# A decode-attention kernel: two ring slots exchanged, the load of x moved to the sync queue, and the last row of W_down read by sixteen small transfers

## The chip, the cores and the metric

The kernel runs on one core of a Trainium2 chip. The metric is device time in microseconds (us), the median of several executions. A profile is one traced execution. Its span (first to last instruction) is 1.8 to 1.9 us shorter than the time of the same execution.

The profile of the kernel before was taken from an execution of 382.86 us, 1.2 us above that kernel's median.

## The reference

One decoding step of a transformer block, with batch 4 and one query token: layer norm of x, a q projection with wq, attention over the last 4096 positions of a K and V cache with 16 KV heads of 128, the output projection wo, and a gated MLP.

```python
W = min(4096, max(256, Sk // 4))                       # 4096
k = jnp.repeat(k_cache[:, :, Sk - W:, :], rep, axis=1) # v likewise
scores = jnp.einsum("bhqd,bhkd->bhqk", q, k) * (Dh ** -0.5)
p = _softmax(scores, axis=-1)
o = jnp.einsum("bhqk,bhkd->bhqd", p, v)
...
h  = x + _A_ref(_layernorm(x), k_cache, v_cache, wq, wo)
h2 = h + _B_ref(_layernorm(h), W_gate, W_up, W_down)   # last product: W_down
```

K and V make 16 tiles each of 4 MB (K0..K15, V0..V15). With the weights, 159.8 MB have to be read. Nothing is read twice.

## The kernel before

A helper records every operation; `P.dma("sync", ...)` issues a load on the sync queue, in program order. K, V and the main part of wq share a ring of four slots of 4 MB. `place` makes a load wait for the last reader of the bytes that it overwrites.

```python
def place(name, off, size, reader, make, key=None):
    deps = []                       # readers of what lay at off..off+size
    ...
    P.dma("sync", ("L",) + name, make, semk, deps)

def add_kv(kind, g):
    s = ring_slot()                 # next of the four slots
    ...
    place((kind, g), off, TILE, ("QK", g, 1) if kind == "K" else ("PV", g), ...)

add_kv("K", 0)                      # slot s
s = ring_slot()                     # slot s+1
place(("wq", 0), wq_off, TILE, "QMM", ...)      # freed by the q projection
P.dma("sync", ("L", "wq", 1), ...)              # wq's last 64 rows, no slot
for g in range(1, NTILE):           # K1, K2, K3 (slot of K0), K4 (slot of wq),
    add_kv("K", g)                  # V0, K5, V1, K6, V2, K7, ...
    if g >= 4:
        add_kv("V", g - 4)
...                                 # wo, W_gate, W_up, V's last tiles
for j in range(4):                  # W_down, 4 blocks of 9 rows per partition
    for r0, r1 in ((0, 9),) if j < 3 else ((0, 6), (6, 9)):
        place(("wd", j, r0), ...)
...
P.dma("scalar", ("L", "x"), lambda e: e.dma_start(out=x_bf[:, :], in_=A_x...), "d_x")
dve("bn0", bn_stats of x_bf)        # waits for x
...                                 # layer norm, transposes of x, xnT
turn_k(0, 0)                        # VectorE transposes the two halves of K0
turn_k(0, 1)
pe_q(); act_q(); dve_q(); put_q(0)  # q projection; q copied where QK reads it
```

VectorE executes in program order (QK(g) are the score matmuls of tile g, PV(g) those with V): in e8, below, K0's first transpose is put ahead of the layer norm and runs at 13.18 us, while the second, behind it, runs at 27.62. So x's layer norm stands ahead of the transposes of K0, these ahead of the copy of q, and that ahead of the first score matmuls QK(0). QK(0) releases K0's slot.

Of the kernel before, what the change touches and what calls it, by code (L numbers as in the profile page):

```python
# [12 lines left out]
D = 576  # L13
# [107 lines left out]
def bass_sequential_preLN__sliding_block_cached__glu_gated_reglu__decode_kernel(  # L121
# [12 lines left out]
    with ExitStack() as es:  # L134
        cnt = [0]

        def sb(name, shape, dt):
            return es.enter_context(nc.sbuf_tensor("sb_" + name, shape, dt))

        P = Prog()  # L140
# [7 lines left out]
        arena = sb("arena", [128, AW], BF16)  # L148
# [23 lines left out]
        x_bf = sb("x_bf", [B, D], BF16)  # L172
# [47 lines left out]
        def place(name, off, size, reader, make, key=None):  # L220
            deps = []
            for blk in range(off // 64, (off + size) // 64):
                r = owner.get(blk)
                if r is not None and r not in deps:
                    deps.append(r)
                owner[blk] = reader
            semk = key or "d_" + "_".join(str(v) for v in name)
            P.dma("sync", ("L",) + name, make, semk, deps)
            land[name] = off

        ring = [(-1 - 2 * NTILE) % NSLOT]

        def ring_slot():
            s = ring[0] % NSLOT
            ring[0] += 1
            return s


        def add_kv(kind, g):
            b, qd = divmod(g, 4)  # L240
            s = ring_slot()
            off = slot0 + s * TILE
            cache = A_k_cache if kind == "K" else A_v_cache
            src = cache[b, 4 * qd:4 * qd + 4, SK - WIN:SK, :].rearrange("a (p t) d -> p a (t d)", p=32)
            place((kind, g), off, TILE, ("QK", g, 1) if kind == "K" else ("PV", g),
                  lambda e: e.dma_start(out=arena[:, off:off + TILE], in_=src), key=f"slot{s}")


        def main_rows(W):
            return W[0:512, :].rearrange("(p r) n -> p (r n)", r=4)  # L250

        def last_rows(W):
            return W[512:576, :].rearrange("r (a n) -> (r a) n", a=2)

        add_kv("K", 0)
        s = ring_slot()
        wq_off = slot0 + s * TILE
        place(("wq", 0), wq_off, TILE, "QMM",
              lambda e: e.dma_start(out=arena[:, wq_off:wq_off + TILE], in_=main_rows(A_wq)), key=f"slot{s}")
        P.dma("sync", ("L", "wq", 1), lambda e: e.dma_start(out=pT[:, 0:2048], in_=last_rows(A_wq)), "d_wq1")  # L260
        for g in range(1, NTILE):
            add_kv("K", g)
            if g >= 4:
                add_kv("V", g - 4)
# [16 lines left out]
        wd_off = []  # L281
        for j in range(4):
            wd_off.append(off)
            for r0, r1 in ((0, 9),) if j < 3 else ((0, 6), (6, 9)):
                place(("wd", j, r0), off + r0 * D, (r1 - r0) * D, "DOWN",
                      lambda e, off=off, j=j, r0=r0, r1=r1: e.dma_start(  # L286
                          out=arena[:, off + r0 * D:off + r1 * D],
                          in_=B_W_down[j * 1152:(j + 1) * 1152, :].rearrange("(p r) n -> p (r n)", p=128)[:, r0 * D:r1 * D]))
            off += WDJ


        pool("c_idb0", lambda e: e.memset(ident_b[:, :], 0.0))
# [21 lines left out]
                                                in_=c_qm[:, :, :].rearrange("p q (h j) -> p q h j", j=4),  # L314
# [34 lines left out]


        act("warm_sqrt", lambda e: e.activation(out=warm[:, 0:1], in_=eps_c[:, :], func=ACT.Sqrt), ["c_eps"])
        P.dma("scalar", ("L", "x"), lambda e: e.dma_start(out=x_bf[:, :], in_=A_x.rearrange("b s d -> (b s) d")), "d_x")
        for hf in range(2):
            dve(f"bn{hf}", lambda e, hf=hf: e.bn_stats(out=bn[:, hf, :], in_=x_bf[:, hf * 288:(hf + 1) * 288]),
                [("L", "x")] if hf == 0 else [])
# [263 lines left out]
        for a in range(8):  # L619
            for j in range(4):  # L620
                for n in range(2):
# [7 lines left out]
                                             in_=bass.AP(tensor=psb, offset=512 + 224, ap=[[4096, 128], [1, 64], [0, 2]])), ["part1"])  # L629
# [28 lines left out]
        for g in range(2):  # L658
            for c in (4, 0, 1, 2, 3):
                off = gu_off[(g, c // 4)]  # L660
                for m in range(3):
                    for j in range(4):
                        first = m == 0 and j == 0 and c % 4 == 0
# [30 lines left out]
        for j in range(4):  # L694
            wv = arena[:, wd_off[j]:wd_off[j] + WDJ].rearrange("p (r n) -> p r n", n=D)
            for r in range(9):
                for n in range(4):
                    deps = []
                    if n == 0 and (r == 0 or (j == 3 and r == 6)):
                        deps = [("L", "wd", j, r)] + (["HC0", "HC1", "HC2"] if j == 0 else [])  # L700
                    pe("DOWN", lambda e, j=j, r=r, n=n, wv=wv: e.matmul(  # L701
                        bank[0][32 * n:32 * n + 32, 0:144], lhsT=hhT[:, r * 128 + 32 * j:r * 128 + 32 * j + 32],
                        rhs=wv[:, r, 144 * n:144 * (n + 1)], start=False, stop=(j == 3 and r == 8), skip_group_check=True), deps)
        dve("OUT", lambda e: e.tensor_copy(out=out_sb[:, :], in_=bank[0][:, 0:144]), ["DOWN"])
        orow = out.rearrange("b s d -> (b s) d")
        for n in range(4):
            P.dma("sync" if n % 2 == 0 else "scalar", ("O", n),
                  lambda e, n=n: e.dma_start(out=orow[:, 144 * n:144 * (n + 1)], in_=out_sb[32 * n:32 * n + 4, :]), f"d_out{n}", ["OUT"])
# [30 lines left out]
```

## Time and profile before

| what | before |
|---|---|
| time | 381.62 us (381.42 to 381.76, 3 executions) |
| bytes read | 159.8 MB at a mean of 419 GB/s |
| steady rate | 432 GB/s, one 4 MB tile every 9.71 us |
| x landed, QK(0) began | 2.4 us, 31.35 us |
| last W_down transfer landed on its last engine | 377.55 us of a span of 381.1 |

From the page of the kernel before: the span, TensorE's granted clock (as a share of full speed) in tenths, the DMA engines' busy share in tenths, and what they moved, each in 40 slices of 9.5 us, and the line of the load queue.

```profile
span 381.1 us, 3671 instructions
PEclk9998999989978897798997887989989956756687
DMA  8999999999999999999999999999999999999993
GB/s 331 440 423 421 406 440 437 433 428 427 420 439 440 424 433 426 433 430 435 433 430 427 435 430 423 435 433 433 430 428 433 427 439 430 423 435 427 419 414 123
q1 hardware_dynamic: 6352, 159.59, 97.7%
```

No slice between the first and the last is below 406 GB/s. The load queue (q1) holds the sixteen engines for 97.7% of the span. The DMA bounds this kernel, and what costs time is a microsecond in which an engine has nothing to do (in e2, below, 12.2 to 12.4 us of bytes are lost, and 12.8 us of time).

From the timeline of the kernel before, the sync queue's issues: start, duration, line, destination and source. A line with x4 merges four issues; most of its duration is waiting.

```profile
0.74 0.63 SPq L246 DMA_DIRECT2D sb_arena<-in_A_k_cache_dram  x1
...
2.51 38.77 SPq L246 DMA_DIRECT2D sb_arena<-in_A_k_cache_dram  x4
53.90 0.54 SPq L246 DMA_DIRECT2D sb_arena<-in_A_v_cache_dram  x1
...
88.36 0.54 SPq L246 DMA_DIRECT2D sb_arena<-in_A_k_cache_dram  x1
97.43 0.54 SPq L246 DMA_DIRECT2D sb_arena<-in_A_v_cache_dram  x1
```

The x4 are K1 and K2 (issued at once), K3 (40.09) and K4 (40.67); then come V0, K5, V1, K6 at 88.36 and V2 at 97.43. V2's data begin to flow at about 101.7, when K6's first engine is done, so its issue is some 4 us ahead. By the same reading the lead is 3 us for K3, 12 for K4, 9 for V0 and 4 for K6.

Now VectorE and TensorE at the start of the kernel before, from the timeline:

```profile
11.19 0.80 DVE L354 BATCH_NORM_STATS2 sb_bn<-sb_x_bf 4x6 f32<-4x288 bf16 x2
...
14.59 14.69 DVE L432 STREAM_TRANSPOSE sb_arena<-sb_arena 128x4096 f32<-128x4096 f32 x2
29.25 0.68 DVE L409 CAST sb_q_keep<-psb 32x512 bf16<-32x512 f32 x1
```
```profile
31.35 5.91 PE L450 MATMUL psb<-sb_arena 128*128 128x512 bf16 x19 [2.14 <-ACT sb_arena L418]
```

The chain can be read off: layer norm at 11.19 (x had long landed, at 2.4; VectorE was held by its constants, which Pool makes: 7.22 us of waiting before 10.79), K0's two transposes from 14.59, the copy of q at 29.25, QK(0) at 31.35.

And the end, from the timeline:

```profile
376.55 1.86 PE L701 MATMUL psb<-sb_arena,sb_pp 128*32 128x144 bf16 x36 [1.31 <-DMA sb_arena<-in_B_W_down_dram]
...
378.45 0.31 DVE L704 CAST sb_out_sb<-psb 128x144 bf16<-128x144 f32 x1 [6.54 <-PE psb L701]
```

The last 12 of these 36 matmuls wait for the last W_down transfer (377.55 on its last engine). Two pieces of the chain of waits (start, length, what) are the load of K7 and that of the end:

```profile
104.42 19.58 DMA sb_arena<-in_A_k_cache_dram
...
344.28 33.27 DMA sb_arena<-in_B_W_down_dram
```

### The profile page before, as it was taken

What the parts mean: (1) busy time and instruction counts of PE and PEld (TensorE: products, weight loads), DVE (VectorE), ACT (ScalarE), POOL (GpSimd) and SP (SyncE); (2) the same over time, 40 slices, a digit from 0 to 9 for tenths busy, and PEclk for the clock granted to TensorE, in tenths of its full rate; (3) what the DMA queues carried; (4) which work ended last, traced back from release to release, by engine and by line L of the source; (5) the groups of instructions that cost most, each with busy time, mean ns of one, the idle gap of its engine ahead of it and who ended that gap; (6) DMA issues with size and microseconds to landing.
All of it is one profiled execution on the core that took longest, in us unless ns stands there. A gap on an engine that the chain in (4) does not pass through costs nothing.

```text
span 381.1 us, 3671 instructions
## 1 busy us (share of the span) xinstructions
PE 278.0 (73%) x1629; PEld 92.8 (24%) x1629; DVE 223.2 (59%) x157; ACT 37.5 (10%) x95; POOL 16.3 (4%) x38
## 2 busy tenths in 40 slices
PE   0057999989959892979996939899969537036544
PEld 0013223322222221222221212222212213015322
DVE  0796799979383917965828279756464455002210
ACT  1112000015000006000000051000000340000100
POOL 8800000000000000000000000000000000000000
PEclk9998999989978897798997887989989956756687
DMA  8999999999999999999999999999999999999993
GB/s 331 440 423 421 406 440 437 433 428 427 420 439 440 424 433 426 433 430 435 433 430 427 435 430 423 435 433 433 430 428 433 427 439 430 423 435 427 419 414 123
DMA packets 6390, 159.81 MB, mean 419 GB/s; under 512 B 740, under 2 KB 744, under 8 KB 1384
## 3 DMA queue, kind: packets, MB, share of 16 engines
q1 hardware_dynamic: 6352, 159.59, 97.7%
q8 instruction: 12, 0.20, 0.2%
q14 instruction: 2, 0.02, 0.0%
q10 hardware_dynamic: 24, 0.01, 0.0%
HBM read 159.58 MB, written 0.00 MB: 419 GB/s over the span
## 4 chain that ended last, share of the span: by engine, by line
PE 44%; DMA 34%; DVE 15%; POOL 2%; ACT 2%; issue 1%; SPq 0%; POOLq 0%
PE psb L450 38%; DMA sb_arena<-in_A_k_cache_dram 19%; DVE sb_arena L432 11%; DMA sb_arena<-in_B_W_down_dram 9%; DMA sb_arena<-in_A_v_cache_dram 7%; PE psb L497 5%; POOL sb_arena L303 2%; ACT sb_pp L475 2%; DVE sb_o_sel L509 1%; DVE sb_o_tmp L505 1%; DVE sb_pp L484 1%; PE psb L534 0%; ACT sb_arena L418 0%; SPq L286 0%; PE psb L469 0%
## 5 line engine op out<-in xcount | busy, mean ns | idle before, releaser
L450 PE MATMUL psb<-sb_arena 128*128 128x512 bf16 x512 | 209.1, 578 | 10.5 <-DVE sb_arena L432 8.2
L432 DVE STREAM_TRANSPOSE sb_arena<-sb_arena 128x4096 f32<-128x4096 f32 x32 | 156.1, 4901 | 48.5 <-DMA sb_arena<-in_A_k_cache_dram 48.4
L450 PEld LDWEIGHTS psb<-sb_arena 128*128 128x128 bf16 x512 | 56.8, 114 | 153.6 <-issue 130.3
L497 PE MATMUL psb<-sb_arena,sb_pp 128*32 128x512 bf16 x512 | 35.9, 431 | 23.0 <-DMA sb_arena<-in_A_v_cache_dram 16.5
L475 ACT ACTIVATE sb_pp<-psb,sb_stat 128x512 bf16<-128x512 f32 x32 | 24.9, 847 | 247.8 <-DVE sb_stat L470 247.8
L505 DVE TENSOR_TENSOR sb_o_tmp<-psb,sb_qm 128x512 f32<-128x512 f32 x16 | 10.8, 676 | 27.9 <-PE psb L497 27.9
L497 PEld LDWEIGHTS psb<-sb_arena,sb_pp 128*32 128x32 bf16 x512 | 13.6, 106 | 47.9 <-issue 22.7
L457 DVE TENSOR_REDUCE sb_stat<-psb 128x1 f32<-128x1024 f32 x4 | 4.8, 1211 | 24.2 <-PE psb L450 24.2
L484 DVE STREAM_TRANSPOSE sb_pp<-sb_pp 128x2048 bf16<-128x2048 bf16 x8 | 18.0, 2278 | 1.4 <-ACT sb_pp L475 1.4
L509 DVE TENSOR_REDUCE sb_o_sel<-sb_o_tmp 128x128 f32<-128x512 f32 x16 | 16.6, 1037 | 0.6
L534 PE MATMUL psb<-sb_o_sel,sb_selw 128*32 128x32 f32 x128 | 2.4, 232 | 16.3 <-DVE sb_o_sel L509 16.3
L668 PE MATMUL psb<-sb_arena,sb_hnT 128*32 128x384 bf16 x120 | 7.9, 437 | 6.6 <-DMA sb_arena<-in_B_W_up_dram 4.5
L375 PE MATMUL psb<-sb_ident_b,sb_xn_bf 4*128 4x4 bf16 x4 | 0.3, 172 | 13.7 <-DVE sb_xnd_bf L364 13.7
L388 PE MATMUL psb<-sb_arena,sb_xnT 128*32 128x512 bf16 x32 | 3.6, 631 | 8.9 <-DMA sb_arena<-in_A_wq_dram 8.9
L675 DVE TENSOR_TENSOR sb_pp<-psb,sb_pp 128x384 bf16<-128x384 f32 x3 | 1.5, 551 | 12.6 <-PE psb L668 12.6
L517 PE MATMUL psb<-sb_stat,sb_sameh 128*128 128x1 f32 x8 | 1.8, 292 | 9.1 <-DVE sb_stat L515 9.1
L303 POOL MEMSET sb_arena<- 128x8192 f32 x1 | 6.9, 6925 | 0.0
L475 ACT ACTIVATION_READ_ACCUMULATOR sb_pp<-psb,sb_stat 128x1 f32 x32 | 6.6, 208 | 0.0
L668 PEld LDWEIGHTS psb<-sb_arena,sb_hnT 128*32 128x32 bf16 x120 | 4.2, 124 | 9.7 <-DMA sb_arena<-in_B_W_up_dram 4.8
L534 PEld LDWEIGHTS psb<-sb_o_sel,sb_selw 128*32 128x32 f32 x128 | 1.9, 142 | 17.4 <-DVE sb_o_sel L509 17.4
L701 PE MATMUL psb<-sb_arena,sb_pp 128*32 128x144 bf16 x144 | 3.8, 250 | 3.0 <-DMA sb_arena<-in_B_W_down_dram 2.5
L418 ACT COPY sb_arena<-sb_q_keep 32x128 bf16<-32x128 bf16 x16 | 4.8, 303 | 1.5 <-DVE sb_q_keep L409 1.4
(123 smaller groups left out, 71.9 us busy)
## 6 DMA issues: line engine op xcount, KB each, us to landing
sb_arena<-in_A_k_cache_dram SPq DMA_DIRECT2D x16, 4096.0 KB, 18.9
sb_arena<-in_A_v_cache_dram SPq DMA_DIRECT2D x16, 4096.0 KB, 24.2
sb_arena<-in_A_wo_dram SPq DMA_DIRECT2D x1, 4608.0 KB, 16.0
sb_arena<-in_B_W_gate_dram SPq DMA_DIRECT2D x1, 4608.0 KB, 30.9
sb_arena<-in_B_W_up_dram SPq DMA_DIRECT2D x1, 4608.0 KB, 42.3
sb_arena<-in_A_wq_dram SPq DMA_DIRECT2D x1, 4096.0 KB, 21.5
sb_arena<-in_B_W_down_dram SPq DMA_DIRECT2D x3, 1296.0 KB, 31.1
sb_arena<-in_B_W_down_dram SPq DMA_DIRECT2D x1, 864.0 KB, 32.7
```

The costliest lines, as they stand in the source:

```text
L303: pool("c_qW", lambda e: e.memset(arena[:, 0:2 * QWW].bitcast(FP32), 0.0))
L418: act(("QW", b), lambda e, i=i: e.copy(out=bass.AP(tensor=arena, offset=32 * i * AW + b % 2 * QWW + 32 * i, ap=[[AW, 32], [128, 4], [514, ...
L432: dve(("TRA", g, w), lambda e: e.transpose(out=dst, in_=src), [("L", "K", g)] if w == 0 else [])
L450: pe(("QK", g, w), lambda e, off=off, steps=steps, wo_=wo_, qd=qd, first=first, last=a == cb == 3: e.matmul(bank[SB[b % 2] + w], lhsT=aren ...
L457: dve(("MAX", b), lambda e: e.tensor_reduce(out=stat[:, b, 0:1], in_=s_ps, axis=AX.X, op=ALU.max, negate=True), [("QK", 4 * b + 3, 1)])
L475: act(("EXP", b, w), lambda e, w=w, a=a: e.activation(out=bass.AP(tensor=pp, offset=4096 + a // 2 * 2048 + w * 1024 + a % 2, ap=[[8192, 12 ...
L484: dve(("PTR", b, w), lambda e: e.transpose(out=dst, in_=src), [("EXP", b, w), ("PV", 4 * b - 1) if b else "QMM"])
L497: pe(("PV", g), lambda e, j=j, tq=tq, k=k: e.matmul(o_ps[32 * j:32 * j + 32, :], lhsT=pT[:, qd * 1024 + tq * 32:][:, 0:32], rhs=v[:, tq * ...
L505: dve(("OS", g), lambda e: e.tensor_tensor(out=o_tmp[:, :].rearrange("p (t d) -> p t d", t=4), in0=o_ps.rearrange("p (t d) -> p t d", t=4) ...
L509: dve(("OSEL", g), lambda e: e.tensor_reduce(out=o_sel[:, qd, :], in_=o_tmp[:, :].rearrange("p (t d) -> p d t", t=4), axis=AX.X, op=ALU.ad ...
L534: pe(("OT", b), lambda e, q=q, qd=qd: e.matmul(ot_ps[32 * qd:32 * qd + 32, 0:32], lhsT=selw[:, qd, 32 * q:32 * q + 32], rhs=o_sel[:, qd, 3 ...
L668: pe(("GU", g, c // 4), lambda e, g=g, m=m, j=j, lo=lo, c=c: e.matmul(bank[3 * g + m][32 * j:32 * j + 32, 0:384], lhsT=hnT[:, c if c < 4 e ...
```

## The change

It consists of three parts. wq takes the slot that K0 had and K0 that of wq; so K3 waits for the q projection and K4 for QK(0), not the other way round. x is loaded on the sync queue behind K0 and wq, not on the scalar queue. The last of the nine rows of W_down's last block is read by 16 transfers of 8, 1, 2, ..., 15 partitions, so that the engines share that last piece differently.

```diff
+        first = ring[0]
+        ring[0] = first + 1
         add_kv("K", 0)
+        ring[0] = first
         s = ring_slot()
         ... place(("wq", 0)) and wq's last rows ...
+        P.dma("sync", ("L", "x"), lambda e: e.dma_start(out=x_bf[:, :], in_=A_x.rearrange("b s d -> (b s) d")), "d_x")
+        ring[0] = first + 2
@@ W_down
-            for r0, r1 in ((0, 9),) if j < 3 else ((0, 6), (6, 9)):
+            for r0, r1 in ((0, 9),) if j < 3 else ((0, 5), (5, 8)):
+        p0 = 0
+        for k in (8,) + tuple(range(1, 16)):
+            ... dma of row 8, partitions p0..p0+k, all on the semaphore "wlast" ...
+            p0 += k
@@
-        P.dma("scalar", ("L", "x"), lambda e: e.dma_start(out=x_bf[:, :], in_=A_x.rearrange("b s d -> (b s) d")), "d_x")
@@ down projection
-                    if n == 0 and (r == 0 or (j == 3 and r == 6)):
+                    if n == 0 and (r == 0 or (j == 3 and r in (5, 8))):
```

More of the change, by code (lines that the diff above doesn't have):

```diff
@@ L289, in bass_sequential_preLN__sliding_block_cached__glu_gated_reglu__decode_kernel @@
             off += WDJ
+        p0 = 0
+        for k in (8,) + tuple(range(1, 16)):
+            (P.dma if p0 else place)(*((("wd", 3, 8), wd_off[3] + 8 * D, D, "DOWN") if not p0 else ("sync", ("L", "wd", 3, 8))),
+                  lambda e, p0=p0, k=k: e.dma_start(
+                      out=arena[p0:p0 + k, wd_off[3] + 8 * D:wd_off[3] + 9 * D],
+                      in_=B_W_down[3456:4608, :].rearrange("(p r) n -> p (r n)", p=128)[p0:p0 + k, 8 * D:9 * D]), "wlast")
+            p0 += k
         pool("c_idb0", lambda e: e.memset(ident_b[:, :], 0.0))
```

## The prediction

> **What bounds it now.** The DMA queue: 159.8 MB at a mean 419 GB/s, the sync queue taking 97.7% of 16 engines' span (queue table). The span ends with the last W_down transfer landing at 377.55 us (chain of waits), 12 matmuls (0.83 us), a copy, the output. Between 3 and 373 us the engines never run dry: the fastest engine lands 4 MB tiles every 9.71 us. The last transfer lands on the first engine at 373.2, on the last at 377.55.
>
> Early issues on the sync queue (timeline): K3 at 40.1 us (freed by QK(0)), V0 53.9, K5 64.3, V1 74.6, K6 88.4, V2 97.4; the data for them are wanted about 2.5 to 8 us after each.
>
> **What the change does.**
> 1. x moves behind K0, wq and wq's last rows on the sync queue. [...] the trace agrees (landings in order of issue). So x lands at about 24.2 us (wq's last rows land 23.7 to 24.2) instead of 2.4. VectorE runs in program order: layernorm of x (bn_stats to xT took 3.4 us, from 11.2) stands before the two K0 transposes (14.7 us) and q's copy. They ran 14.6 to 29.3; they will run 27.6 to 42.3. QK(0) starts at 44.4 instead of 31.35: 13 us later. PE and VectorE were busy without a gap from 31 to 75-80 us (K1 to K4), so this delay is not absorbed there.
> 2. Exchanged slots: K3 waits for the q projection (about 32 us) instead of QK(0); K4 for QK(0). This saves K3, not the later ones. K4 is issued at about 53.2 (data wanted from 52.5), V0 67, K5 77.4, V1 87.8, K6 98.9, V2 108.8 (estimates from the trace's block times: 6.9 us per QK half, 3.5 for the other layout, 1.84 per PV). The queue runs dry several times. Restart from an idle queue costs about 2.2 us before full rate (K0: issue at 0.74, landing 12.7 to 13.3). V2 lands at about 121.2 instead of 113.1; from K7 on the ring has slack again and the delay stays: about +8.4 us.
> 3. Last row: 128 packets of 1152 B (about 50 ns each). [...] Issuing 15 more is hidden: the queue is 30 us ahead. The last PE wait shrinks from 12 to 4 matmuls, but the row before lands almost together. Net -0.1 to -0.5 us.
>
> **Predicted:** 390.0 us, 80% range 387.0 to 392.0. Faster by over 2% 0.01; within 2% 0.34; slower 0.65.
>
> **What would show it.** x landing near 24; VectorE idle until then after its constants; first K0 transpose near 27.6; QK(0) near 44.4; throughput dips in slices between 50 and 110 us, none later; K3 issued near 32; V2's landing 8 us later.
>
> **What would make it wrong.** x overtaking the loads (then about 381); restarts dearer than 2.2 us under load (391-392) or cheaper (388.5); another distribution of the slow engines' delays (instruction fetches of 16 KB cost one engine 1.5 us each), worth 1 us either way.

Its sum: 381.6 us before, plus 8.4 for the late x with the exchanged slots, less 0.1 to 0.5 for the last row, is 389.5 to 389.9. For the order within a queue the trace before suffices: the tiles from K3 to K7 landed in the order of their issue (53.09 to 123.99 us). The net of the last row stands as my estimate, from the packets' 50 ns and the 0.83 us of the 12 matmuls; how the row's packets fall on the engines was not shown. Of "busy without a gap" that trace shows TensorE's matmuls unbroken from 31.35 to 75.47 us, and VectorE's transposes from 44.98 to 79.8, after waits of 3.24 and 2.23 us.

## The result, and the profile after

| | before | after |
|---|---|---|
| time, median | 381.69 us (381.42 to 382.25, 4) | 394.21 us (393.68 to 395.61, 4) |
| ratio | | 1.0332 [1.0301, 1.0363], slower |
| x landed | 2.4 us | 24.16 us |
| QK(0) began | 31.35 us | 44.07 us |
| V2 landed on first..last engine | 111.38..113.09 | 121.80..124.84 |

A ratio is the mean time of one kernel's runs over that of the other's of the same rounds, so it is not quite the ratio of the medians. Here the change costs 12.5 us by the medians; 8.4 had been predicted. Landings are the times at which the engines completed a transfer, from the trace's records of semaphores.

The same lines of the page, after. A slice is now 9.8 us.

```profile
span 392.7 us, 3687 instructions
PEclk9998599999996999698999896989996957756595
DMA  7999966999999999999999999999999999999993
GB/s 320 427 434 441 452 277 267 427 377 412 377 377 439 434 431 431 430 434 421 429 434 431 434 432 434 427 426 434 434 426 427 434 437 377 433 423 433 422 416 128
q1 hardware_dynamic: 6616, 159.59, 95.6%
```

The bytes are the same and the rate is about 430 in most slices, as before. The sixth and seventh slice (49 to 69 us) fell to 277 and 267, and four of the next five (to 118 us) are below 415. The loss is in the first 118 us. One smaller dip comes much later (377, at about 325 us): the load of wo waits for PV and is issued at 325.66, when the first engine is about to run out (325.80). The last engine loses nothing there. It landed the tile ahead at 330.32 and wo at 341.24, 10.92 us later, which is the steady time of wo's 4.5 MB. What remains is the tail.

The issues of the sync queue after, from the timeline:

```profile
2.51 0.49 SPq L264 DMA_DIRECT2D sb_x_bf<-in_A_x_dram  x1
3.04 51.26 SPq L246 DMA_DIRECT2D sb_arena<-in_A_k_cache_dram  x4
67.57 0.54 SPq L246 DMA_DIRECT2D sb_arena<-in_A_v_cache_dram  x1
...
99.48 0.54 SPq L246 DMA_DIRECT2D sb_arena<-in_A_k_cache_dram  x1
109.44 0.53 SPq L246 DMA_DIRECT2D sb_arena<-in_A_v_cache_dram  x1
```

The x4 are again K1, K2, K3 (32.06, earlier than before) and K4, whose issue is at 53.76, when the queue is running dry: K3 landed between 52.92 and 54.48. V0's issue at 67.57 comes after K4 had landed on all engines (66.10).

VectorE and TensorE at the start, after:

```profile
24.18 0.81 DVE L365 BATCH_NORM_STATS2 sb_bn<-sb_x_bf 4x6 f32<-4x288 bf16 x2 [12.80 <-DMA sb_x_bf<-in_A_x_dram]
...
27.46 14.69 DVE L443 STREAM_TRANSPOSE sb_arena<-sb_arena 128x4096 f32<-128x4096 f32 x2
41.99 0.66 DVE L420 CAST sb_q_keep<-psb 32x512 bf16<-32x512 f32 x1
```
```profile
44.07 7.28 PE L461 MATMUL psb<-sb_arena 128*128 128x512 bf16 x21 [10.31 <-ACT sb_arena L429]
```

Every line is 12.7 to 13.0 us later than its partner. The layer norm has 12.80 us of waiting in front of it, released by the load of x. The chain of waits says the same and shows the tail too:

```profile
2.51 21.65 DMA sb_x_bf<-in_A_x_dram
...
44.07 49.38 PE psb L461 x140
...
116.43 18.11 DMA sb_arena<-in_A_k_cache_dram
...
373.09 16.62 DMA sb_arena<-in_B_W_down_dram
389.75 0.34 PE psb L712 x4
```

x is 4.6 KB and takes 21.65 us to land, since it queues behind 8.9 MB. The piece at 116.43 is K7: it lands at 134.54, against 124.00 before. And the end, from the timeline:

```profile
388.89 0.55 PE L712 MATMUL psb<-sb_arena,sb_pp 128*32 128x144 bf16 x12 [0.23 <-DMA sb_arena<-in_B_W_down_dram]
389.75 0.31 PE L712 MATMUL psb<-sb_arena,sb_pp 128*32 128x144 bf16 x4 [0.32 <-DMA sb_arena<-in_B_W_down_dram]
390.12 0.31 DVE L715 CAST sb_out_sb<-psb 128x144 bf16<-128x144 f32 x1 [9.07 <-PE psb L712]
```

Only 4 matmuls wait for the last row, as intended, but that row is 0.9 us behind rows 5 to 7 (388.84 and 389.71).

The landings of the early tiles show how the delay builds up. Times are in us; "issue to first, to last" is from the issue to the landing on the first and on the last engine.

| tile | before: landing, first..last | after: issue | after: landing, first..last | after: issue to first, to last |
|---|---|---|---|---|
| K3 | 53.09..54.79 | 32.06 | 52.92..54.48 | 20.9, 22.4 (queued) |
| K4 | 62.82..64.52 | 53.76 | 65.76..66.10 | 12.0, 12.3 |
| V0 | 72.53..74.24 | 67.57 | 79.25..80.02 | 11.7, 12.5 |
| K5 | 82.23..83.95 | 77.94 | 89.91..90.91 | 12.0, 13.0 |
| V1 | 91.96..93.66 | 88.31 | 100.02..101.81 | 11.7, 13.5 |
| K6 | 101.66..103.37 | 99.48 | 111.56..115.16 | 12.1, 15.7 |
| V2 | 111.38..113.09 | 109.44 | 121.80..124.84 | 12.4, 15.4 |
| K7 | 121.10..123.99 | 116.43 | 131.52..134.54 | 15.1, 18.1 (queued) |

From K7 on the tiles come every 9.71 us in both kernels: the delay stays, 10.4 to 10.5 us on the first engine, up to the last V tile before wo (325.80 against 315.35). Summed over the packets, the kernel after is 10.2 to 10.5 us of bytes behind from 110 to 310 us (of the kernel before), and 11.5 after the dip at wo. On the last engine it is 10.55 us at K7 and 11.3 at the last transfer of several rows (388.84 against 377.55).

### The profile page after: what moved, and what is told of

Its sections match the earlier page's. It is cut to its first block, busy times and chain, and to the rows that moved or that the text cites. A ratio compares the mean times of both kernels' runs of the same rounds, so it can differ in the third digit from the quotient of the medians.

```text
span 392.7 us, 3687 instructions
## 1 busy us (share of the span) xinstructions
PE 277.4 (71%) x1629; PEld 92.8 (24%) x1629; DVE 223.0 (57%) x157; ACT 37.5 (10%) x95; POOL 16.0 (4%) x38
## 4 chain that ended last, share of the span: by engine, by line
PE 48%; DMA 29%; DVE 14%; SPq 5%; ACT 2%; issue 1%
PE psb L461 41%; DMA sb_arena<-in_A_k_cache_dram 13%; DVE sb_arena L443 10%; DMA sb_arena<-in_A_v_cache_dram 6%; DMA sb_x_bf<-in_A_x_dram 6%; PE psb L508 5%; DMA sb_arena<-in_B_W_down_dram 4%; SPq L298 4%; ACT sb_pp L486 2%; DVE sb_o_sel L520 1%; DVE sb_o_tmp L516 1%; DVE sb_pp L495 1%; SPq L291 0%; PE psb L480 0%; PE psb L545 0%
## 5 line engine op out<-in xcount | busy, mean ns | idle before, releaser
L516 DVE TENSOR_TENSOR sb_o_tmp<-psb,sb_qm 128x512 f32<-128x512 f32 x16 | 10.8, 675 | 27.6 <-PE psb L508 27.6
L508 PEld LDWEIGHTS psb<-sb_arena,sb_pp 128*32 128x32 bf16 x512 | 13.6, 105 | 48.0 <-issue 22.0
L365 DVE BATCH_NORM_STATS2 sb_bn<-sb_x_bf 4x6 f32<-4x288 bf16 x2 | 0.8, 438 | 12.8 <-DMA sb_x_bf<-in_A_x_dram 12.8
L686 DVE TENSOR_TENSOR sb_pp<-psb,sb_pp 128x384 bf16<-128x384 f32 x3 | 1.5, 551 | 10.2 <-PE psb L679 10.2
```

The costliest lines, as they stand in the source:

```text
L508: pe(("PV", g), lambda e, j=j, tq=tq, k=k: e.matmul(o_ps[32 * j:32 * j + 32, :], lhsT=pT[:, qd * 1024 + tq * 32:][:, 0:32], rhs=v[:, tq * ...
L516: dve(("OS", g), lambda e: e.tensor_tensor(out=o_tmp[:, :].rearrange("p (t d) -> p t d", t=4), in0=o_ps.rearrange("p (t d) -> p t d", t=4) ...
```

## The experiments

The theory after the result: x alone makes the delay; the exchange gives a part of it back, less than predicted, because a restart (the first tile after the queue has run dry, or nearly so) lands later on some engine than a tile queued behind others; the small transfers do little. Rivals: the exchange itself does harm; the small transfers, which take the sync engine 17 us to issue, make the difference; x's queue matters, not its place in it; the loss comes from the end and not from the start.

Unless said otherwise each diff is against the kernel before, and all results were correct.

### One part at a time

**e1_slots_only**: the exchange alone.

```diff
+        first = ring[0]
+        ring[0] = first + 1
         add_kv("K", 0)
+        ring[0] = first
         s = ring_slot()
...
+        ring[0] = first + 2
```

> Before plus the exchanged ring slots alone. My theory (late x delays QK(0), the delay makes the load queue run dry): K3 is issued near 27 us instead of 40 because it waits for the q projection, K4 near 40; no wait ends later, so 381.0 to 381.9, at most 0.3 us faster. Rival A (the exchange itself hurts, because K4 now waits for QK(0)): over 384.

Measured: 381.37 us, ratio 0.9994 [0.9982, 1.0006]. K3 was issued at 27.52 instead of 40.09, yet landed at 53.06..54.71 against 53.09..54.79: it had to wait for its turn in the queue either way. The exchange alone neither helps nor harms.

**e2_x_only**: x on the sync queue behind wq's last rows, nothing else.

```diff
         P.dma("sync", ("L", "wq", 1), ...)
+        P.dma("sync", ("L", "x"), ...)
...
-        P.dma("scalar", ("L", "x"), ...)
```

> Before plus x on the sync queue alone, slots not exchanged, old last transfers. My theory: QK(0) starts near 44, K3 waits for it and is issued near 53.7 with its data wanted from 42.7, so the queue is dry for 12 us at once; 395 to 398, that is worse than the whole change. If late x were harmless (rivals A or B): under 384.

Measured: 394.52 us, ratio 1.0331 [1.0315, 1.0347]: 12.8 us, 0.5 below the range expected. QK(0) began at 44.35, and K3, which now waits for it, was issued at 53.81. The rate row of its page (a slice is 9.8 us):

```profile
GB/s 320 427 434 434 149 160 427 427 434 439 431 427 429 427 431 441 430 431 431 429 434 434 427 429 431 431 432 431 437 429 431 434 437 431 421 430 411 437 414 158
```

There is one hole, in the fifth and sixth slice (39 to 59 us), and nothing is lost after it: the packets are 12.2 to 12.4 us behind from then to the end. K3 took 11.9 to 12.3 us from issue to landing, and K4 was issued 0.6 us after it, so the queue was filled again. The model of the prediction (the issue by the block times, 12.0 to 12.4 us from issue to landing after an empty queue, 9.71 per further tile) gives the landings of this case right.

**e4_x_and_slots**: both edits above, the old tail.

> The changed kernel with the old last transfers of W_down. My theory: 392 to 394, QK(0) near 44, dry spells between 52 and 112 us as in the changed kernel, the end about 1 us earlier than its 394.2. Rival B: near 382.

Measured: 393.12 us (391.14 to 393.89), ratio 1.0289 [1.0265, 1.0313]. Its rate row:

```profile
GB/s 321 438 432 431 431 286 284 381 394 376 371 391 433 428 432 431 437 435 435 426 428 435 431 430 431 431 423 438 431 430 431 438 428 417 427 441 415 435 408 164
```

The exchange splits one deep hole into two slices of 285 and then five of 371 to 394. In sum it saves 1.4 us of e2's 12.8. V1, K6 and V2 landed on their last engines 15.7, 14.8 and 14.7 us after their issue.

**e3_tail_only**: the sixteen small transfers alone.

```diff
-   ... else ((0, 6), (6, 9)):
+   ... else ((0, 5), (5, 8)):
+   # row 8 by 16 transfers of 8, 1, 2, ..., 15 partitions
```

> Before plus the last row in 16 small transfers alone. My theory: the completions of one engine's small transfers come about 0.17 us apart, the engine that is last has a handful of them, so 0 to 1 us slower: 381.6 to 382.8. Rival B (the 16 transfers are most of the loss: the chain of waits of the changed kernel gives 4% of the span to issuing them): over 386.

Measured: 382.97 us, ratio 1.0027 [1.0011, 1.0044], just above the range expected. By the ratio it is slower by 1.0 us, not faster. Its six times lie in two groups, 381.92 and 381.97, and 382.66 to 383.57. In the trace the last data packet ended at 376.65, but the completions of the last engine's small transfers came one by one, 0.20 us apart, up to 378.82.

**e12_slots_and_tail**: exchange and tail, x as before.

> The changed kernel with x back on the scalar queue: the other two parts together. The sum of their separate ratios is 0.9994 + 0.0027: 381.9 to 383.3. QK(0) at 31.4. If the exchanged slots mattered to the loss beyond x: over 385.

Measured: 382.80 us (381.68 to 383.26), ratio 1.0018 [0.9999, 1.0036]; two groups again. With e3 it shows that the long issue of the sixteen transfers on the sync engine does no harm by itself: in both, the last data packet ended within 0.9 us of where it ended with the old tail (376.65 and 376.26; 375.80 in e1, 377.15 before).

**e7_row_one_transfer**: the last row in one transfer of 128 partitions instead of sixteen.

```diff
-   for k in (8,) + tuple(range(1, 16)):
+   for k in (128,):
```

> Before with the last row of W_down in one 128-partition transfer of its own (the chunks of the changed kernel, without the 16 small transfers). Theory C (one engine's small transfers complete one after another, 0.17 to 0.2 us each, and the last engine held 5 to 13 of them): one completion per engine, so the loss is gone: 381.2 to 382.0. Rival D (1152-byte packets or the extra waits of PE cost): 382.7 to 383.3 as the 16 transfers alone.

Measured: 382.31 us, ratio 1.0019 [1.0006, 1.0031], slightly above the 381.2 to 382.0 of the expectation. By the times (0.7 us by the ratio) it cannot be told from e3, so they do not separate the number of transfers from the extra piece. The table under "The tail in the traces" below tells them apart.

**e9_rows_119**: with the exchange, the last three rows in transfers of 119, 7 and 2 partitions, an idea meant to spare the engine that ends last its packets of these rows. Which engines serve such transfers, and which engine ends last, I had assumed. The "low engine" is one that I assumed to serve them. No trace shows the numbers of the engines.

> Exchanged slots, and the last three rows of W_down in 3 transfers of 119, 7 and 2 partitions instead of 1 of 128. [...] its 8 packets of 135 ns (1.06 us) go, 380.2 to 381.0. If an instruction fetch makes a low engine the last one: 381.5 to 382.5. [...]

Measured: 384.11 us, ratio 1.0061 [1.0048, 1.0073]. The idea failed: an engine that carried 18 packets of 135 ns (an even share of the 128 packets over sixteen engines is 8) began them only at 375.79 and ended at 378.17. So a late engine had been given more of these packets, not fewer.

### x's place, and VectorE's order

**e6_x_mid**: the exchange, and x on the sync queue between K0 and wq.

```diff
         add_kv("K", 0)
+        P.dma("sync", ("L", "x"), ...)
         ring[0] = first
```

> Exchanged slots, old last transfers, x on the sync queue but between K0 and wq, so that it lands near 13.4 us. My theory: QK(0) starts about 2 to 3 us later than before (near 34), which the ring's slack of 2.5 us and more absorbs: 381 to 383. If the sync queue itself were the trouble for x (rival), it would be near the 393 of x late.

Measured: 381.77 us, ratio 1.0002 [0.9988, 1.0016]. The layer norm started at 13.35, QK(0) at 33.40. That is 2 us later than before, and costs nothing, since K4 is still issued 11 us before its data can flow (41.79 and 52.89). So it is not the sync queue as such, but the 8.9 MB in front of x.

**e8_transpose_first**: e4 with VectorE's order changed: the first transpose of K0, which does not need x, ahead of x's layer norm.

```diff
+        turn_k(0, 0)
         for hf in range(2):
             dve(f"bn{hf}", ... bn_stats of x ...)
...
         dve_x()
-        turn_k(0, 0)
         turn_k(0, 1)
```

> x as late as in the change (behind wq), slots exchanged, old last transfers, but the first of the two K0 transposes stands before the layernorm of x in VectorE's program. x still lands near 24.2. My theory (what costs is that the K0 transposes wait behind x in VectorE's order): QK(0) near 37.2 instead of 44, end at 383 to 387. If the late x cost by the late q projection alone: near 393 as e4.

Measured: 385.76 us, ratio 1.0101 [1.0085, 1.0118]. From its timeline:

```profile
13.18 7.43 DVE L364 STREAM_TRANSPOSE sb_arena<-sb_arena 128x4096 f32<-128x4096 f32 x1 [1.79 <-DMA sb_arena<-in_A_k_cache_dram]
24.36 0.81 DVE L369 BATCH_NORM_STATS2 sb_bn<-sb_x_bf 4x6 f32<-4x288 bf16 x2 [3.75 <-DMA sb_x_bf<-in_A_x_dram]
27.62 7.42 DVE L364 STREAM_TRANSPOSE sb_arena<-sb_arena 128x4096 f32<-128x4096 f32 x1
```
```profile
36.89 9.32 PE L454 MATMUL psb<-sb_arena 128*128 128x512 bf16 x32 [3.39 <-ACT sb_arena L433]
```

x is as late as after the change (24.36), but QK(0) is 7.5 us earlier than e4's 44.41, about the length of the transpose moved (7.43), and the time falls by 7.4 us. This shows how x's lateness reaches the time: through VectorE's program order, the transposes of K0 and QK(0). An exposed microsecond there is a microsecond at the end. The rest is the part that the lead of the queue does not cover: K6 and V2 still took 15.1 and 15.2 us from issue to their last landing.

### What a restart costs

**e10_restart_full**: the kernel before, but K8, V4, K9, V5, K10 and V6 are each issued only after the tile ahead has landed on all engines.

```diff
+            chain = [("V", 3), ("K", 8), ("V", 4), ("K", 9), ("V", 5), ("K", 10), ("V", 6)]
+            if name in chain[1:]:
+                deps.append(("L",) + chain[chain.index(name) - 1])
```

> A measurement of the disputed cost by itself: the kernel before, where the issue of each of K8, V4, K9, V5, K10, V6 also waits until the transfer ahead of it has landed on all 16 engines. Six restarts of a fully empty queue. By the single dry spell of x alone (issue to last landing about 12.4 us) each 4 MB transfer takes 12.4 to 12.6 us instead of 9.71, V6 lands near 209 instead of 192, and the end is 16 to 18 us later: 397 to 400. If a restart cost only its latency of 1.4 us: about 393.

Measured: 400.12 us, ratio 1.0481 [1.0453, 1.0508]. Issues from its timeline:

```profile
132.67 0.54 SPq L249 DMA_DIRECT2D sb_arena<-in_A_k_cache_dram  x1
145.05 0.54 SPq L249 DMA_DIRECT2D sb_arena<-in_A_v_cache_dram  x1
```

The issues are 12.4 us apart (the next comes at 157.49), and a tile takes 12.0 us to its first engine and 12.3 to 12.4 to its last, once 13.6. The time is just above the range expected. After a truly empty queue a tile costs 2.3 to 2.7 us above the steady 9.71 and the engines mostly stay together. This is the figure that the prediction had used. The 1.4 us of the expectation are K0's in the kernel before: issued at 0.74, first packet at 2.15.

**e11_restart_engine0**: the same, but each waits only for a one-partition marker behind the tile ahead. Such a marker (128 B) runs on one engine: the six of them add 12 packets to the load queue (6364, against 6352 in e10), one of data and one of completion each. The other fifteen may still be busy.

```diff
+                deps.append(("M", chain.index(name) - 1))
...
+                P.dma("sync", ("M", i), lambda e: e.dma_start(out=scr[0:1, 64 * i:64 * i + 64], in_=A_x[0, :, 0:64]), "mk")
```

> The same six issues, but each waits for a one-partition marker queued behind the transfer ahead, so for one engine alone [...] to have emptied its queue; the other engines may still be busy. If a restart beside busy engines costs what a restart from empty costs: issue to last landing 12 to 13 us and an end like that of the full restarts or up to 3 us earlier. If it is what made V1, K6 and V2 of the changed kernel late on some engines (13.5 to 15.7 us from issue to last landing): 14 us and more here too, and an end later than that of the full restarts.

Measured: 396.81 us, ratio 1.0394 [1.0370, 1.0418]. The result is mixed. The end came 3.3 us earlier than in e10, not later, so the branch with the later end missed: the overlap gains more than the unevenness costs. But single tiles behave otherwise than in e10: to the first engine 11.8 to 12.2 us, to the last 14.2, 14.9, 15.9, 12.9, 13.5 and 12.3. Beside engines that are still busy, a restart leaves the last engine up to 3.5 us behind the 12.4 of a clean one. So three of six such restarts were uneven (14.2 us and more to the last engine) and three were not (12.3 to 13.5): being issued beside busy engines makes a late engine possible, not certain. A finer version, waiting for half of a tile's completions, was not tried.

### The same kernels again

**e13_whole_again**: the changed kernel, unaltered, in a later session.

> The changed kernel again, as the reference for the two beside it on the same chip: 393.5 to 395 us.

Measured: 393.20 us (391.31 to 394.15), ratio 1.0299 [1.0280, 1.0318], just below the range expected.

**e14_x_and_slots_again**: e4 once more, in the same session.

> The changed kernel with the old last transfers. Theory: the last-row part costs about 1 us in the changed kernel as it does alone (ratio 1.0027): 392.3 to 393.8, 0.5 to 1.5 us below the whole change. By my prediction's term (last row 0.1 to 0.5 us faster) it would be the slower of the two.

Measured: 392.71 us, ratio 1.0282 [1.0262, 1.0301].

**e15_whole_one_transfer**: the changed kernel with its last row in one transfer.

> The changed kernel with the last row in one 128-partition transfer instead of 16 small ones. If the small transfers' completions in a row (0.17 to 0.2 us each on one engine) carry the cost: 0.4 to 1 us below the whole change. If the extra chunk carries it: like the whole change.

Measured: 392.59 us, ratio 1.0281 [1.0262, 1.0299]. The three intervals overlap; by the times the tail is worth about 0.6 us here and its sign is not settled. The traces of the five executions with a late x and exchanged slots say more about the main term:

| traced execution | its time | K6, V2: issue | V2: issue to last landing | V2: last landing | K7: first..last landing |
|---|---|---|---|---|---|
| predicted | 390.0 | 98.9, 108.8 | 12.4 | 121.2 | |
| e13 (changed kernel again) | 391.31 | 98.36, 108.33 | 12.9 | 121.21 | 130.22..131.96 |
| e15 | 392.48 | 98.66, 108.63 | 15.3 | 123.96 | 130.86..133.63 |
| e14 | 393.00 | 99.53, 109.50 | 15.4 | 124.88 | 131.49..134.43 |
| e4 | 393.89 | 99.97, 109.93 | 14.7 | 124.58 | 132.42..135.49 |
| after | 394.65 | 99.48, 109.44 | 15.4 | 124.84 | 131.52..134.54 |

The traced execution of e13 is the same program as "after", and it behaved as predicted: V2 at 121.21, and 391.31 us, within the range. In the other four an engine was 2.3 to 3.0 us beyond the 12.4 at V2. The prediction had described the best of this kernel's nine executions, not their median.

What the difference looks like in the packets of the kernel after, as the number of DMA engines busy (counted from the trace's packets, each figure the mean of the half microsecond that begins there), around the landing of V1 and the start of K6 (issued at 99.48):

```
us      99.5  100.0  100.5  101.0  101.5  102.0  102.5  103.0  103.5
busy    14.8    8.5    4.4    8.3   14.7   15.0   15.0   15.1   16.0
```

The engines run out one after the other and start again one after the other. From 101.5 to 103.4 fifteen are busy and one is idle. Its first packet of K6 then starts at 103.43 and takes 2.47 us, against 1.20 to 1.24 for most packets of that size. In e13's trace K6 was issued at 98.36, and all sixteen were busy again from 100.7. In e4's, three packets that started between 102.0 and 103.1 took 3 us each. The idle engine is not one that was late at V1: the engine that ended V1 last ran to 101.53 and went on without a pause, so a lag carried over from an instruction fetch (there was one at 93.71) is not the reason. Why one engine is held back, and not another, no view of the profile shows.

### The tail in the traces

For each traced execution two intervals can be read: from the end of the last W_down data packet to the last completion that TensorE waits for, and from the last landing of K7 to the end of the (timed) execution, which takes the start of the kernel out.

| last row read by | traces | data end to last completion, us | K7's last landing to end, us |
|---|---|---|---|
| a chunk of 3 rows, as before | before, e1, e4, e14 | 0.40, 0.45, 0.40, 0.41 | 258.87, 258.64, 258.40, 258.57 |
| one transfer of 128 partitions | e7, e15 | 0.45, 0.65 | 258.86, 258.85 |
| 16 transfers | e3, e12 | 2.17, 2.21 | 260.49, 260.44 |
| 16 transfers | after, e13 | 1.06, 1.38 | 260.11, 259.35 |

All six traces without the small transfers are at 258.4 to 258.9 (as are e2, e6 and e8, which have the old chunk: 258.58 to 258.79), all four with them at 259.3 to 260.5. On average the chunk stands at 258.62, one transfer at 258.86 and the sixteen at 260.10: 1.5 us dearer than the chunk, and 0.2 for one transfer. In e3 and e12 the packets that ended last were a row of 11 or more last-row packets back to back (51 ns each); in the kernel after and e13 a row of 5. The last completion follows the last packet by about 0.2 us for each (11 x 0.20 is 2.2, measured 2.17 and 2.21; 5 x 0.20 is 1.0, measured 1.06, and 1.38 in e13). So in these traces the first interval goes with the number of transfers on the late engine. It is not all of the 1.5 us: in the kernel after, the data themselves also ended later after K7's last landing (254.11 us, against 253.16 before and 253.20 in e13), and why is not shown. The timed means give less, 0.7 (e12) to 1.0 us (e3), because some executions, those of the lower group, show no loss. No such execution was traced, so what they do differently stays open.

## Why the prediction was wrong

The prediction was 390.0 us, with 387.0 to 392.0. The median is 394.21, and 393.20 in the repetition.

**The path was right, step by step.** Predicted and measured: x lands at about 24.2 (24.16); K0's transposes 27.6 to 42.3 (27.46 to 42.15); QK(0) at 44.4 (44.07); K3 issued near 32 (32.06); K4 53.2 (53.76); V0 67 (67.57); K5 77.4 (77.94); V1 87.8 (88.31). The throughput dips between 50 and 118 us (50 and 110 had been predicted, and none later; the dip at 325 us cost nothing), and the delay then stays. That x queues behind K0 and wq is what the trace shows: K0 landed at 12.8 to 13.2, wq's main part at 22.5 to 22.9, its last rows at 23.78 to 24.14 and x at 24.16. e2, e6 and e8 show the path itself.

**The step that failed: "Restart from an idle queue costs about 2.2 us before full rate (K0: issue at 0.74, landing 12.7 to 13.3). V2 lands at about 121.2 instead of 113.1".** The mechanism (the queue runs dry, and each restart costs more than a queued tile) was right, and the size of this term was off. In the prediction's sum a restart takes 12.4 us from issue to last landing, 2.7 more than the steady 9.71. V2 took 15.4, which is 5.7 more. The 2.2 us came from the one restart that the trace before holds, K0's, where all engines start empty; e10 confirms it for that case (2.3 to 2.7). In the changed kernel, K5 to V2 are each issued 0.5 to 2.1 us before the tile ahead lands on its first engine, so most engines are still busy. V2 landed at 124.84, which is 3.6 us later than predicted. The prediction had named this as its weak point ("restarts dearer than 2.2 us under load (391-392)"), but gave it 1 to 2 us. The 3.6 us are 0.6 from the issue (109.44 for 108.8) and 3.0 from issue to last landing (15.4 for 12.4).

Put otherwise, the prediction had credited the idle stretches with letting the late engine catch up: the 1.7 us between first and last engine at V2 before (111.38 to 113.09) would have shrunk to 0.4. It grew to 3.0. From there it did not all reach the end against the profile of before, because there an engine lost another 1.2 us at K7 (19.6 us from issue to last landing, 16.7 to the first; the trace has an instruction fetch at 113.49 and fifteen engines busy from 113.50 to 114.55). Against e1, a typical execution of the old timing (K7 at 122.73), K7 is 11.8 us late. The two traced executions add up so: V2 11.75 us later than before, less 1.20 at K7, plus 1.24 in the tail is 11.79, and 394.65 less 382.86 is 11.79.

**The 0.6 us of the issue differ from execution to execution.** K4 waits for QK(0), and QK(0) began at a reduced clock, 0.50. TensorE had been idle for 10.31 us before it. From the stage table of the kernel after (the third last column is the granted clock, the last GB/s):

```profile
36.00:42.00 6.00, 0.00 (x0) 0.00 (x0) 6.00 (x2) 0.00 (x0) 0.00 (x0) 0.50 1.01 437
42.00:48.00 6.00, 3.93 (x10) 1.46 (x11) 6.00 (x11) 2.45 (x8) 0.00 (x0) 0.50 1.01 434
48.00:54.00 6.00, 6.00 (x26) 2.39 (x25) 6.00 (x2) 0.00 (x0) 0.00 (x0) 0.89 0.63 268
```

The granted clock was 0.50 from 36 to 48 us, and the first half of QK(0) took 6.0 us instead of 5.1. In e13 the same stages were granted 0.56, 0.59 and 1.00, and K4 was issued at 52.64 instead of 53.76, before the 53.2 of the prediction. So this term is a matter of the moment, worth half a microsecond either way. The prediction had carried over a QK(0) from a trace in which TensorE waited only 2.14 us, and was granted 0.72 from 30 to 36 us and 1.00 from 36 to 54. The wait alone does not decide it: in e13 it was 10.31 us too, and the first half of QK(0) took 4.8 us, less than the 5.1 before. What sets the clock in that moment is not shown.

**The last row.** The prediction's "Net -0.1 to -0.5 us" has the wrong sign: plus 1.5 us in the traced executions, plus 0.6 to 1.0 in the timed means (where e12's interval just includes zero). It counted packets (50 ns each), and those are right: 51 ns, and the last engine carried 5, where an even share of the 128 is 8. What it left out is that each small transfer completes by itself on each engine that it uses. The page of the kernel after has 868 packets under 512 B, that of the kernel before 740: the 128 data packets of the last row brought 128 completions of 4 B, where a transfer of 128 partitions brings 16. The traces of e3, e12 and the kernel after give the price that the prediction lacked, 0.17 to 0.20 us for each completion in a row (the first interval above is 0.7 to 1.8 us longer than with the old chunk). That the matmuls behind the last wait fell from 12 to 4 was right, and saved less.

**The exchange** was sized wrongly by the same step. Set against the 12.8 us measured for x alone, the prediction's 8.4 gives it about 4 us; measured are 1.4 (e4) to 1.8 us (e14). It does what it was meant to do, filling the hole from 44 to 54 us with K3, but the five tiles that follow (V0, K5, V1, K6, V2) are then each issued to a queue that has run dry or is about to, and each pays part of a restart, where e2 pays once and in full.

**The rivals.** The exchange does no harm (e1, 0.9994). The small transfers' long issue does no harm (e3, e12). The sync queue as such does no harm (e6, 1.0002). "The loss comes at the end" fails for all but the tail's microsecond: the byte count is 10.2 us behind at 116 us.

**What stays open.** Why single engines start late in a restart beside busy ones, and in which executions; the five traced executions show it in four. The prediction's range was too narrow on the upper side for the same reason: this kernel spreads from 391.31 to 395.61 in its nine executions, the kernel before from 381.28 to 382.93 in some forty, and the range had been built from one trace of a kernel that never restarts. No version tried beats the kernel before; e1 and e6 equal it. For the instruction fetches the prediction had allowed 1 us either way, at 1.5 us each. The traces before and after show 12 fetches of 16384 B each, of 0.89 to 1.11 us; during the one at 113.49 before, fifteen engines moved data, so it took one of the sixteen. One fetch put the last engine 1.2 us (K7 before) to 1.5 us further behind (the tile that landed at 262.33 after).

## What to carry to other kernels

A load of 4.6 KB is worth as much as what waits for it: behind 8.9 MB on a queue that is never empty it lands 21.65 us after its issue, and an engine that works in program order passes the delay on to work that never needed it. On a queue with little lead (3 to 12 us here) a later release becomes a restart. Size a restart by how the transfers of the kernel at hand land on the last engine, not by the start of the program; here several half-empty restarts (e4, 11.4 us) were about as dear as one hole (e2, 12.8). Splitting a last transfer to spread its bytes adds one completion per piece and engine (128 here, 16 for one transfer), and at the end of this kernel these cost more than the bytes saved (the sixteen pieces stood 1.5 us above the chunk in the traces).
